# Banded attention and two gated layers on one core: units 8 to 15 of the attention planned 3.5 positions apart instead of 4

## The chip, the cores and the metric

The kernel runs on one core of one Trainium2 chip, in one launch. The metric is device time in microseconds (us): the median of several runs of the whole kernel. One further execution was taken by the hardware profiler, and all rows below come from that one. PE is the matrix engine, PEld its weight loads, DVE the vector engine, ACT the scalar engine, POOL the engine for general work, SP the engine that issues the DMAs.

## The reference

```
k_sum = k.reshape(B, H, nb, 32, D).max(axis=3)
v_sum = v.reshape(B, H, nb, 32, D).mean(axis=3)
scores = concat(where(|i - j| < 16, scale * q @ k.T, -1e9), scale * q @ k_sum.T + log(32))
x = softmax(scores) @ concat(v, v_sum)
x = x.transpose(0, 2, 1, 3).reshape(1536, 512)
x = ((x @ w_a) * (x @ w_b)) @ w_out
h = x @ w_in
out = (h - tanh(h)) @ w_out2
```

B is 2, H 8, S 768 and D 64; the first layer has 1536 inner columns, the second 2048. All is float32.

## The kernel before

**Attention.** The 1536 rows are cut into 24 units of 64 queries, 12 for each batch, all heads at once. A unit goes through T1 (the queries are transposed on PE, line 269, and copied to `qbd` by ACT, line 273), W (its keys are copied, line 280), T2 (scores on PE, line 288; mask and row minimum on DVE, line 299; exponent on ACT, line 303), T2b (normalisation: lines 314, 315 and 317 on DVE for odd units, line 320 on ACT for even ones), T3 (transpose on PE, line 327, copy by ACT, line 330) and T4 (weighted values on PE, line 340; the result is split in a high and a low part by ACT, line 347, and DVE, line 348). Eight units make one block of 512 rows, which the first layer takes as its input tile `XA` (blocks 0 and 2) or `XB` (block 1). Units 0 to 7 run in a hand-written head, units 8 to 15 during block 0 of the first layer, units 16 to 23 during block 1.

**The first layer.** Its work is a list `pos` of positions, 36 for each block. A position is one weight tile of 128 rows by 512 and twelve matmuls: `pos_a` (tile `pa`, line 370, copied to `ta` by ACT, line 378), `pos_b` (tile `pb`, line 370; product `tg` on DVE, line 386; then `gh` on ACT, line 363, and `gl` on DVE, line 364) and `pos_o` (line 398, into four accumulators `acc`). Their order is a0, b0, a1, b1, o0, a2, b2, o1 and so on, and o10, o11 at a block's end. In block 0 position j is the first to use weight j. Of a position's twelve matmuls, some need only the high part of the weight (written by ACT, line 184), the others also the low part (DVE, line 185).

**Weights.** In block 0 every weight is loaded, decoded and split. `load_next` issues a 512 KB load from SP (lines 141 and 143) into one of five staging buffers; `dec_a` reads it on ACT (lines 154 and 155), POOL clamps (line 179), `dec_b` finishes on DVE (lines 161, 164 and 165), and with that the buffer is free and the load of the weight five further on is issued. `split_w` writes the two parts (lines 184 and 185).

**What sets the order.** `plan(j, fn, ...)` hangs a step on position j, and `run_plan(j)` calls it just ahead of that position. From position 0 on, a scheduler orders PE, DVE, ACT and POOL, and calls with T1, T2, T2b, T3, T4, W and `prep_k` in them get a higher priority; SP alone keeps the order in which the steps are called (`REG`). The values of a unit live in three rotating buffers `vw`: with T4 of unit u the plan also calls `load_v(u + 3)` (line 258), which writes the buffer that T4 of unit u reads, so this load waits for that T4, and whatever SP has behind it waits too. `mean_v` (line 240, copied by ACT, line 245) is planned at position 13, the transposes of the second batch's keys (`prep_k`, line 223) at positions 1 to 11.

Of the kernel before, what the change touches and what calls it, by code (L numbers as in the profile page):

```python
# [39 lines left out]
def band_attention_moe_kernel(ctx: ExitStack, tc: tile.TileContext, q, k, v, w_a, w_b, w_out, w_in, w_out2, out):  # L40
# [168 lines left out]
    def where(u):  # L209
        b, w = divmod(u, S // 64)  # L210
        return b, w, min(max(w * 64 - WIN, 0), S - KW)
# [266 lines left out]
    groups, begin, pos = [], {}, []  # L478
# [41 lines left out]
    def plan(j, fn, *args):  # L520
        at.setdefault(j, []).append((fn, args))
# [27 lines left out]
    plan(VM + NC + 4, mean_v, "pt")  # L549
    OFF = -2  # L550
    for n, u in enumerate(range(8, 24)):
        j = (n - 8) * 4 + begin[1] + OFF if n >= 8 else n * (begin[1] // 8) + OFF
        b, w, _ = where(u)
        if u % 2 == 0:
            m = u // 2
            if m + 2 < 12:
                plan(j, load_q, m + 2)
            plan(j, T1, m, "pt", qbd)
            if u >= 12:
                plan(j, W, u)  # L560
                plan(j, W, u + 1)
        if u % 8 == 0:
            plan(j, new_x, u // 8)
        plan(j + 2, T2, u, "ps")
        plan(j + 3, T2b, u)
        plan(j + 5, T3, u, "pt")
        plan(j + 7, T4, u, "ps")
        if u + 3 < 24:
            plan(j + 7, load_v, u + 3)
            if 12 <= u + 3 < 15:  # L570
                plan(max(j + 7, VM + NC + 5), load_vm, u + 3)
# [263 lines left out]
```

## Time and profile before

| what | value |
|---|---|
| median of 3 runs | 660.51 us (659.32 to 661.34) |
| profiled execution, its own time | 659.97 us |
| span in the profile | 658.2 us |
| PE busy | 637.4 us, 97% of the span |
| DVE, ACT and POOL busy | 501.9, 475.1 and 209.1 us |
| granted PE clock, mean | 0.995 |

The span runs from the first instruction to the last; the profiled execution's time holds 1.8 us more, around the span. Matmuls overlap one another, so a busy share of PE near 100% says that PE had work, not that it ran at its peak. A row of the timeline gives the start, the duration, the engine, the line, and in brackets how long the engine stood idle before it and what ended that.

### The profile page before, as it was taken

The page shows a single profiled execution, that of the slowest core. Times are in us where ns is not written, and L with a number is a line of the kernel's source. Part 1 is how long each engine was busy: PE and PEld are TensorE (multiplying, and loading weights), DVE is VectorE, ACT ScalarE, POOL GpSimd, SP SyncE. Part 2 cuts the span into 40 slices and gives each one's busy share as a digit, 9 for nine tenths or more (in the row PEclk, how much of TensorE's full clock was granted, in tenths as well). Part 3 has the DMA queues.
Part 4 walks back from the last instruction along what each step waited for, and adds up shares of the span by engine and source line. Part 5 has one row for each costly group of instructions (what it writes and reads, how often), then busy time and mean ns, then how long its engine had stood idle before and what let it go on. Part 6 is the DMA issues. An engine that isn't in the chain of part 4 may idle for free.

```text
span 658.2 us, 9626 instructions
## 1 busy us (share of the span) xinstructions
PE 637.4 (97%) x3240; PEld 518.2 (79%) x3240; DVE 501.9 (76%) x999; ACT 475.1 (72%) x1000; POOL 209.1 (32%) x221
## 2 busy tenths in 40 slices
PE   7779999999799999999999999999999999999997
PEld 5567876888588888888888888888888888888885
DVE  5889999898675777747877749777777877777775
ACT  4899886897686787645655548777777777777774
POOL 6752231222000011100111134554444554444441
PEclk9979999999999999999999999999999999999999
DMA  9996984563324554513444200000010000010001
GB/s 203 242 240 185 249 224 127 176 214 116 81 89 124 164 161 141 154 54 113 143 145 145 80 1 0 1 0 1 1 64 1 0 1 0 26 40 1 1 0 64
DMA packets 84781, 62.11 MB, mean 94 GB/s; under 512 B 51892, under 2 KB 75444, under 8 KB 84732
## 3 DMA queue, kind: packets, MB, share of 16 engines
q1 hardware_dynamic: 84732, 61.50, 33.3%
q8 instruction: 25, 0.41, 0.3%
q14 instruction: 24, 0.20, 0.1%
HBM read 54.00 MB, written 7.34 MB: 93 GB/s over the span
## 4 chain that ended last, share of the span: by engine, by line
PE 83%; DVE 8%; ACT 4%; DMA 2%; issue 2%; SPq 1%; POOL 0%; DVEq 0%; ACTq 0%
PE acc L459 20%; PE pb L370 18%; PE pa L370 17%; PE acc L398 12%; PE pt L370 5%; PE ps L370 5%; PE ps L288 1%; DVE w L164 1%; PE ps L340 1%; DVE wsp L185 1%; DMA stage<-in_moe_w_in_dram 1%; DVE w L165 1%; PE pt L240 1%; PE pt L327 1%; SPq L610 1%
## 5 line engine op out<-in xcount | busy, mean ns | idle before, releaser
L185 POOL TENSOR_TENSOR wsp<-w,wsp 128x512 fp32r<-128x512 f32 x97 | 127.4, 1330 | 140.0 <-ACT wsp L184 140.0
L184 ACT ACTIVATE wsp<-w 128x512 fp32r<-128x512 f32 x201 | 121.3, 622 | 17.8 <-PE acc L398 8.0
L185 DVE TENSOR_TENSOR wsp<-w,wsp 128x512 fp32r<-128x512 f32 x104 | 73.9, 712 | 41.0 <-ACT wsp L184 40.8
L179 POOL TENSOR_SCALAR w<-w 128x512 f32<-128x512 f32 x52 | 41.8, 809 | 181.7 <-ACT w L154 168.9
L398 PE MATMUL acc<-gh,wsp 128*128 128x512 f32 x288 | 96.5, 394 | 1.2 <-ACT gh L363 1.2
L370 PE MATMUL pa<-XA,wsp 128*128 128x512 f32 x336 | 85.2, 402 | 2.1 <-ACT XA L720 2.1
L370 PE MATMUL pb<-XA,wsp 128*128 128x512 f32 x336 | 83.9, 393 | 1.4 <-DVE tg L386 1.4
L459 PE MATMUL acc<-wsp,gh 128*128 128x512 f32 x256 | 78.8, 389 | 0.0
L370 PEld LDWEIGHTS pa<-XA,wsp 128*128 128x128 f32 x336 | 64.1, 193 | 16.6 <-ACT XA L720 2.4
L370 PEld LDWEIGHTS pb<-XA,wsp 128*128 128x128 f32 x336 | 62.1, 188 | 14.9 <-ACT x21a L155 1.7
L363 ACT ACTIVATE gh<-tg 128x512 fp32r<-128x512 f32 x68 | 42.4, 624 | 33.9 <-DVE tg L386 33.6
L398 PEld LDWEIGHTS acc<-gh,wsp 128*128 128x128 f32 x288 | 53.7, 188 | 11.9 <-ACT gh L363 1.3
L370 PE MATMUL pb<-XB,wsp 128*128 128x512 f32 x240 | 60.8, 396 | 0.0
L370 PE MATMUL pa<-XB,wsp 128*128 128x512 f32 x240 | 60.0, 394 | 0.0
L398 PE MATMUL acc<-gl,wsp 128*128 128x512 f32 x144 | 56.8, 396 | 1.1 <-DVE gl L364 1.1
L459 PEld LDWEIGHTS acc<-wsp,gh 128*128 128x128 f32 x256 | 48.1, 188 | 9.9
L364 DVE TENSOR_TENSOR gl<-tg,gh 128x512 fp32r<-128x512 f32 x68 | 46.8, 688 | 9.1 <-ACT gh L363 8.9
L370 PEld LDWEIGHTS pa<-XB,wsp 128*128 128x128 f32 x240 | 44.5, 188 | 9.4 <-DVE XB L348 0.2
L370 PEld LDWEIGHTS pb<-XB,wsp 128*128 128x128 f32 x240 | 44.4, 188 | 9.2
L459 PE MATMUL acc<-wsp,gl 128*128 128x512 f32 x128 | 49.8, 389 | 0.0
L459 PE MATMUL acc<-wsp,vw 128*128 128x512 f32 x192 | 46.5, 391 | 0.0
L459 PEld LDWEIGHTS acc<-wsp,vw 128*128 128x128 f32 x192 | 35.9, 188 | 8.2 <-ACT vw L363 0.4
(304 smaller groups left out, 1175.5 us busy)
## 6 DMA issues: line engine op xcount, KB each, us to landing
stage<-in_moe_w_out_dram SPq DMA_DIRECT2D x19, 512.0 KB, 3.5
stage<-in_moe_w_in_dram SPq DMA_DIRECT2D x16, 512.0 KB, 5.6
stage<-in_moe_w_a_dram SPq DMA_DIRECT2D x8, 512.0 KB, 5.0
w<-wsc SPq DMA_DIRECT2D x16, 256.0 KB, 3.4
vw<-in_v_dram SPq DMA_DIRECT2D x19, 192.0 KB, 3.0
stage<-in_moe_w_b_dram SPq DMA_DIRECT2D x7, 512.0 KB, 5.6
wsc<-x21a SPq DMA_DIRECT2D x8, 256.0 KB, 5.1
wsc<-x21b SPq DMA_DIRECT2D x8, 256.0 KB, 4.9
```

The source lines that it names most:

```text
L164: nc.vector.scalar_tensor_tensor(r, t[:, :, 1], -0x40000000, r, op0=ALU.bitwise_and, op1=ALU.bitwise_or)
L165: nc.vector.tensor_tensor(r, r, t[:, :, 0], op=ALU.add)
L179: nc.gpsimd.tensor_scalar(rf, rf, HI_HI, HI_LO, op0=ALU.min, op1=ALU.max)
L184: nc.scalar.activation(s[:, 0, :], r, AF.Copy)
L185: eng.tensor_tensor(s[:, 1, :], r, s[:, 0, :].bitcast(F32), op=ALU.subtract)
L240: mm(pp, mavg[:, NB - 4 - 4 * c : 2 * NB - 4 - 4 * c], vch.pop(c).rearrange("p h d -> p (h d)"), start=(c == 0), stop=(c == NC - 1),)
L288: mm(pp[:, p, 0:NK], qt[:, p, :], kw[:, p, :], start=True, stop=True)
L363: nc.scalar.activation(dst[0], src, AF.Copy)
L364: eng.tensor_tensor(dst[1], src, dst[0].bitcast(F32), op=ALU.subtract)
L370: mm(dst, w, xx, start=(kk == 0 and n == 0), stop=(kk == KC - 1 and n == 2))
L398: mm(acc[blk][d][:, c0:c1], w, t, start=(f == 0 and c0 == 0 and n == 0), stop=(f == F1 - 1 and n == 2))
L459: mm(a[c], g[:, cs], s[:, i, :], start=(f == 0 and n == 0), stop=(f == F2 - 1 and n == 2))
```

## The change

Only the position at which the steps of units 8 to 15 are hung changes. `begin[1]` is 36, so the step between them was 36 // 8, that is 4. It is now 3.5, rounded down.

```diff
     OFF = -2
     for n, u in enumerate(range(8, 24)):
-        j = (n - 8) * 4 + begin[1] + OFF if n >= 8 else n * (begin[1] // 8) + OFF
+        j = (n - 8) * 4 + begin[1] + OFF if n >= 8 else n * 7 // 2 + OFF
         b, w, _ = where(u)
```

The starts of units 8 to 15 were -2, 2, 6, 10, 14, 18, 22 and 26; they are now -2, 1, 5, 8, 12, 15, 19 and 22. T2 stands 2 positions after a unit's start, T2b 3, T3 5, T4 and `load_v(u + 3)` 7; T1, W and `load_q` stand at the start. Units 16 to 23 and all else keep their positions.

**SP, loads from the values of unit 14 on.** Rows with `vw<-in_v_dram` are `load_v`; the rows with `moe_w_a`, `moe_w_b` and `moe_w_out` are weights in the order of positions, Before:

```order
L258 DMA vw<-in_v_dram 96x8x64
L263 DMA vw<-w 24x512
L141 DMA stage<-in_moe_w_b_dram 128x4x256
L143 DMA x21a<-in_moe_w_out_dram 128x1024
L141 DMA x21b<-in_moe_w_a_dram 128x4x256
L141 DMA stage<-in_moe_w_b_dram 128x4x256
L258 DMA vw<-in_v_dram 96x8x64
L143 DMA stage<-in_moe_w_out_dram 128x1024
L252 DMA qn<-in_q_dram 128x8x64
L141 DMA stage<-in_moe_w_a_dram 128x4x256
L141 DMA x21a<-in_moe_w_b_dram 128x4x256
L143 DMA x21b<-in_moe_w_out_dram 128x1024
```

Now, from the values of unit 15 on:

```order
L258 DMA vw<-in_v_dram 96x8x64
L252 DMA qn<-in_q_dram 128x8x64
L141 DMA x21b<-in_moe_w_a_dram 128x4x256
L141 DMA stage<-in_moe_w_b_dram 128x4x256
L143 DMA stage<-in_moe_w_out_dram 128x1024
L258 DMA vw<-in_v_dram 96x8x64
L141 DMA stage<-in_moe_w_a_dram 128x4x256
L141 DMA x21a<-in_moe_w_b_dram 128x4x256
L143 DMA x21b<-in_moe_w_out_dram 128x1024
L143 DMA stage<-in_moe_w_out_dram 128x1024
L258 DMA vw<-in_v_dram 96x8x64
L141 DMA stage<-in_moe_w_in_dram 128x4x256 x2
```

Before, the weights of positions 27 to 30 stood behind the values of unit 14, and those of 31 to 34 behind the values of unit 15. Now 29, 30 and 31 stand behind the values of unit 15, 32 to 35 behind those of unit 16, and only weights of the second layer (`w_in`) behind those of unit 17.

**PE, around T4 of unit 15 and the start of block 1.** `XA` marks a matmul of block 0, `XB` one of block 1; line 340 is T4, here of unit 15, line 269 is T1 of units 16 and 17. Before:

```order
L398 MATMUL acc_887<-gl,wsp 128x512
L398 MATMUL acc_887<-gh,wsp 128x512
L327 MATMUL pt<-ident,e 120x128 x4
L340 MATMUL ps<-at,vw 64x64 x8
L269 MATMUL pt<-ident,qn 128x128 x4
L370 MATMUL pa<-XB,wsp 128x512
L370 MATMUL pb<-XB,wsp 128x512
```

Now:

```order
L398 MATMUL acc_890<-gl,wsp 128x512
L398 MATMUL acc_890<-gh,wsp 128x512
L327 MATMUL pt<-ident,e 120x128 x4
L370 MATMUL pa<-XA,wsp 128x512 x2
L340 MATMUL ps<-at,vw 64x64 x8
L269 MATMUL pt<-ident,qn 128x128 x4
L370 MATMUL pa<-XA,wsp 128x512 x10
L370 MATMUL pb<-XA,wsp 128x512 x12
L398 MATMUL acc_887<-gh,wsp 128x512
```

Before, the two `pos_o` rows are o11's and T4 of unit 15 is the last thing ahead of block 1. Now they are o9's: T4 of unit 15 stands inside a11 (position 32), with b11 and o10 behind it; o11 itself stands behind block 1's first twelve matmuls.

**ACT, ahead of the copy of T3 of unit 15 (line 330, tile `at`).** Lines 154 and 155 decode a weight, line 184 splits one. Before:

```order
L184 ACTIVATE wsp_1973<-w_1923 128x512
L184 ACTIVATE wsp_1991<-w_506 128x512
L303 ACTIVATE e_1853,sm_1855<-e_1853,nm_1854 128x120 x4
L184 ACTIVATE wsp_2025<-w_533 128x512
L363 ACTIVATE gh_2021<-tg_2019 128x512
L184 ACTIVATE wsp_2052<-w_609 128x512
L347 ACTIVATE XB_671<-ps_1886 128x4x64
L410 ACTIVATE x20a_2067<-acc0_884 128x512
L410 ACTIVATE x20b_2068<-acc2_886 128x512
```

Now:

```order
L154 ACTIVATE w_1883<-x21a_1723 128x512
L155 ACTIVATE x21a_1723<-x21a_1723 128x512
L303 ACTIVATE e_1740,sm_1742<-e_1740,nm_1741 128x120 x3
L154 ACTIVATE w_1905<-x21b_1777 128x512
L155 ACTIVATE x21b_1777<-x21b_1777 128x512
L347 ACTIVATE XB_671<-ps_1809 128x4x64
L363 ACTIVATE gh_1960<-tg_1958 128x512
L154 ACTIVATE w_1942<-stage_1804 128x512
L155 ACTIVATE stage_1804<-stage_1804 128x512
L184 ACTIVATE wsp_1898<-w_1845 128x512
L155 ACTIVATE stage_1843<-stage_1843 128x512
L330 ACTIVATE at_1853<-pt_1848 120x512
```

Before, no weight of the first layer was left to decode when unit 15 came to its T3. Now the decodes of weights 33 (`w_1883`), 34 (`w_1905`) and 35 (`w_1942`) and one instruction of the first second-layer weight (`stage_1843`) stand ahead of that copy, and the split of weight 32 (`w_1845`) behind all three decodes. Ahead of the first row shown stand, from the decode of weight 32 on, lines 154 and 155 (weight 32), 184 (weight 31), 280 and one of line 303.

## Rows read from the trace of the kernel before

**Rows 1.** Busy time by stretch: us, then busy by engine, clock, DMA share, GB/s.

```profile
57.37:116.52 59.15, 59.15 (x317) 45.36 (x318) 54.83 (x118) 48.27 (x110) 14.10 (x16) 1.00 0.76 197
116.52:176.11 59.59, 56.15 (x321) 45.20 (x320) 52.73 (x124) 49.84 (x118) 12.86 (x15) 1.00 0.47 146
178.01:291.97 113.96, 113.96 (x655) 93.49 (x655) 75.81 (x192) 79.74 (x196) 10.61 (x15) 1.00 0.45 133
```

**Rows 2.** Timeline of PE, end of block 0, from T4 of unit 14.

```profile
168.03 0.69 PE L340 MATMUL ps<-at,vw 120*64 120x64 f32 x16
169.93 1.21 PE L398 MATMUL acc<-gh,wsp 128*128 128x512 f32 x4 [1.21 <-ACT gh L363]
...
176.11 0.69 PE L340 MATMUL ps<-at,vw 120*64 120x64 f32 x16 [1.02 <-ACT at L330]
```

**Rows 3.** Chain of waits in order of time: start, us, what.

```profile
60.35 0.44 PE pt L327 x4
64.47 0.88 PE ps L288 x8
71.76 0.62 PE ps L340 x16
97.46 5.26 PE pt L240 x12
163.81 0.47 ACT at L330
176.79 0.59 PE pt L269 x4
177.38 0.40 PE pa L370
191.20 2.72 PE pa L370 x12
```

**Rows 4.** Timeline around T4 of unit 13: PE, SP, ACT.

```profile
154.47 0.69 PE L340 MATMUL ps<-at,vw 120*64 120x64 f32 x16
155.19 0.33 SPq L258 DMA_DIRECT2D vw<-in_v_dram  x1
155.63 0.48 SPq L143 DMA_DIRECT2D stage<-in_moe_w_out_dram  x1
159.71 0.67 ACT L154 ACTIVATE w<-stage 128x512 f32<-128x512 f32 x1 [0.80 <-DMA stage<-in_moe_w_out_dram]
```

**Rows 5.** Timeline: T4 of unit 10, and the first weight behind it.

```profile
109.24 0.69 PE L340 MATMUL ps<-at,vw 120*64 120x64 f32 x16
115.88 0.67 ACT L154 ACTIVATE w<-x21a 128x512 f32<-128x512 f32 x1 [1.92 <-DMA x21a<-in_moe_w_a_dram]
```

**Rows 6.** Timeline of ACT, back to back.

```profile
149.70 0.51 ACT L280 ACTIVATE kw<-kt 128x384 f32<-128x384 f32 x1
150.11 0.62 ACT L184 ACTIVATE wsp<-w 128x512 fp32r<-128x512 f32 x1
150.63 0.65 ACT L154 ACTIVATE w<-x21b 128x512 f32<-128x512 f32 x1
151.19 0.66 ACT L155 ACTIVATE x21b<-x21b 128x512 int32<-128x512 uint32 x1
151.75 0.38 ACT L303 ACTIVATE e<-e,nm 128x120 f32<-128x120 f32 x1
...
153.26 0.57 ACT L378 ACTIVATE ta<-pa 128x512 f32<-128x512 f32 x1
```

**Rows 7.** Timeline of DVE: the low part of T4 of unit 10.

```profile
111.99 0.42 DVE L348 TENSOR_TENSOR XB<-ps,XB 128x256 fp32r<-128x256 f32 x1
```

**Rows 8.** Busy time by stretch of 2 us; the third number from the end is the clock.

```profile
44.00:46.00 2.00, 2.00 (x6) 1.52 (x6) 1.83 (x4) 1.96 (x5) 0.64 (x1) 0.50 1.39 212
168.00:170.00 2.00, 0.79 (x18) 0.62 (x17) 2.00 (x5) 2.00 (x8) 0.00 (x0) 1.00 0.06 15
```

**Rows 9.** Timeline of PE: the first twelve matmuls of block 0.

```profile
42.48 5.74 PE L370 MATMUL pa<-XA,wsp 128*128 128x512 f32 x12 [2.11 <-ACT XA L720]
```

## The prediction

> **What bounds the kernel now.** I began with busy time by stretch [rows 1]. From 178 us on PE is never idle: in 113.96 us it is busy 113.96, and the chain of waits from there to the end is a string of twelves of matmuls at 2.72 us, one like the next [rows 3]. A change to block 0 therefore moves the end by what PE gains or loses before 178 us, and by nothing more, as long as it opens no wait behind that. From 57.37 to 116.52 PE has no idle time either, though DVE is busy 54.83 of 59.15 us. From 116.52 to 176.11 PE is busy 56.15 of 59.59 us, so 3.44 us are lost. The timeline of PE then says where: all of it lies behind T4 of unit 14 [rows 2]. `o11` waits for `gh` and `gl`, which are made late, and then T4 of unit 15, the last thing that block 1 needs, waits 1.02 us for the copy of its T3 on ACT.
>
> The second thing to read is what starts a weight load. T4 of unit 13 starts at 154.47; the load of values that waits for it is issued at 155.19, the next weight right behind it at 155.63, and ACT, which stood idle for it, begins to decode at 159.71 [rows 4]. So SP's weights stand behind a load that waits for a T4, and the first of them is ready 5.24 us after that T4 starts. After T4 of unit 10 the same took 6.64 us [rows 5]. In block 0 PE can run no further than these weights allow.
>
> **What the change does, and the sum.** It removes and adds no instruction. It moves the steps of units 9 to 15 ahead by 1 to 4 positions against the weights, and the built order shows what comes of that on PE, ACT and SP.
>
> *The wait that goes.* From the start of T4 of unit 14 (168.03) to the first matmul of block 1 (177.38) PE takes 9.35 us [rows 2, 3]. Its work there is T4 twice (0.62 each), `o11` (2.72), T3 (0.44) and T1 (0.59), 4.99 us [rows 3], so 4.4 us are lost. The busy row says 3.44 [rows 1]. The Trainium skill (Perfetto Trace Analysis, Identifying the Most-Contended Engine) says that matmul busy time is a poor measure, since matmuls are pipelined. By the busy row my sum would come out 1.0 us higher; the 4.4 counts starts alone, so I take 4.4 and keep 3.4 as the other end. In the new order `o11` stands behind the first twelve matmuls of block 1, which gives `gh` and `gl` 2.72 us more, and T4 of unit 15 stands in `a11` with 22 more matmuls and `o10` between it and block 1. Both old waits go: -4.4 us.
>
> *The wait that comes.* Now look from T4 of unit 13 to T4 of unit 15 in the new PE order. PE's work between them is T4 0.62, `a10` 2.72, T3 0.44, `b10` 2.72, T2 0.88, T4 0.62, `o9` 2.72, T3 0.44 and two matmuls of `a11` 0.45 (2.72 for twelve): 11.6 us [rows 3]. Behind T4 of unit 13 SP now issues weights 32 to 35, and ACT has to have decoded all four before it splits weight 32 and copies T3 of unit 15. The first lands after 5.24 us [rows 4]. Then ACT takes, by the distance of one start to the next [rows 6]: four decodes of 0.56 + 0.56 each, 4.48; two splits at 0.52, 1.04; W 0.41; four exponents 1.51; `gh`, taken as a split, 0.52; line 347, taken as W, 0.41; one more line 155, 0.56; and the copy of T3, 0.47 [rows 3]. That is 9.4 us, so T4 of unit 15 can start 14.6 us after T4 of unit 13, where PE is ready after 11.6: +3.0 us. Part of it will show a little earlier, at the two matmuls of `a11`, for want of the split of weight 32, or at T3, for want of the normalised rows. The low end is 2.8: from 154.47 to 168.03 PE took 13.56 us [rows 2, 4] for work that sums to 13.27 (T4, two matmuls of `b10`, `o9`, `a11`, T3, `b11`, T2, `o10`), so small work between matmuls costs some 0.3. The high end is 4.4, with 6.64 us for the first landing [rows 5].
>
> *A second wait, at weight 22.* Behind T4 of unit 10 SP now has the values, the queries and then weights 22 to 24, four and more positions ahead of their use where weight 23 was six ahead. PE's work from that T4 to `o6` is two T4, T3, T2, and 46 matmuls: 1.24 + 0.44 + 0.88 + 10.43 = 13.0 us. ACT needs 5.24 + 0.44 for one more issue ahead [rows 4], then three decodes 3.36, three splits 1.56 and 0.1 to the end of the last, W 0.41, `gh` 0.52, exponents 1.51, line 347 0.41: 13.6 us. +0.6 us; between 0 (a load ahead of time) and 2.0 (first landing after 6.64).
>
> *Costed at nothing.* The same sum for weight 29 behind T4 of unit 12 leaves 0.7 us to spare; with the late landing of rows 5 that would be 0.7 lost. `mean_v` keeps its 5.26 us [rows 3] but now stands behind eight matmuls of `o4`, and DVE has the low part of T4 of unit 10 ahead of the decode of weight 19: DVE runs out of work some 5 us before that T4, where it reached this row at 111.99 without such a gap [rows 7]. What hides it is that weight 19 is first needed 6 us of PE work behind that T4; by my estimate it is split about 1 us ahead. If that cover is gone, `o5` waits what is over. The copies of T1, W and the query loads move with their unit, in ACT and SP time that is counted above. In block 1 DVE and ACT are busy 75.81 and 79.74 of 113.96 us [rows 1], so units 16 to 23, which keep their positions and start a little earlier on PE, hide as before.
>
> The sum: -4.4 + 3.0 + 0.6 = -0.8 us. The profiled execution took 659.97 us, 0.54 under the median of the runs, and would come to 659.2; for the median that is 660.51 - 0.8 = **659.7 us**. A measurement of this kernel can tell about 0.3% from no change, 2.0 us, so this is no change. By the bounds alone it lies between -4.4 + 2.8 + 0 = -1.6 and -3.4 + 4.4 + 2.0 + 0.7 = +3.7 us.
>
> **Rivals.** *Faster: one wait goes and little comes.* If the weights behind T4 of unit 13 are ready for ACT sooner than one burst behind a T4 has been so far, or ACT stands ahead by a microsecond, the wait at T4 of unit 15 halves to 1.5 us and the one at weight 22 closes: -2.9 us, 657.6. For it: the old loss was at one place alone, and T4 of unit 15 now has more than two positions in hand before block 1. Against it: ACT's row of decodes is fixed by the order, and no burst in these rows landed faster than 5.24 us. Chance 0.25.
>
> *Slower: SP's queue sets the pace.* SP issues a T4's load of values now 1 to 3 weights earlier, so the bursts of weights start with 3 to 6 positions in hand where they had 4 to 7. If the first weight of a burst takes 6.64 us as behind unit 10 [rows 5], all three places lose: 4.4, 2.0 and 0.7 us, against 4.4 or 3.4 gained: at the upper end +3.7 us, 664.2. It decides from new waits of 6.4 us in sum on. For it: ACT stood idle for the first weight of a burst in both bursts shown. Against it: the 6.64 us held a small copy of `mean_v` between, which stands elsewhere now. Chance 0.18.
>
> *Slower: the clock falls.* In the 2 us from 168 PE was busy 0.79 us and the granted clock stayed 1.00, the 2.4 GHz level; at 44 to 46, after the idle time ahead of the first layer, it was 0.50, which is 1.2 GHz [rows 8]. Twelve matmuls took 5.74 us there [rows 9], 3.0 more than 2.72. One such fall at the new wait gives +2.2 us, 662.7. The Trainium skill (TensorE: Matmul & The Clock Gate, The HAM clock gate) has idle time as what brings the lower level; by that rule the new wait of 3 us would be at risk, and the trace, with longer losses at 1.00, speaks against it. Chance 0.03.
>
> **How the numbers follow.** The forecast has 0.54, all of it within 0.3% of 660.51 (658.5 to 662.5); the first rival is the chance of faster, 0.25; the other two that of slower, 0.21. The likeliest time is 659.7. The range is 657.0 to 663.2: it takes in the first rival's 657.6 with some 0.6 us below it for a weight-22 wait that closes with nothing in its place, the bounds of the sum up to +2.7 us, and leaves out the upper third of the queue rival and the tail of the faster one, under 2 in 10 together.
>
> **What would show it.** Right: the two waits of `o11` for `gh` and `gl` are gone; PE waits for ACT at T4 of unit 15, or just ahead of it at `a11` or T3, some 3 us in sum, two twelves and more before the first matmul on `XB`; that first matmul starts between 173 and 176 us with `o11` still to come; DVE shows a gap of about 5 us ahead of a row of line 348 near 106 to 111 us; SP's weight loads still follow a load of values by 0.4 us; the clock stays 1.00; from 178 us on PE has no idle time. Wrong: no wait of PE over 1.5 us in 150 to 176 (the faster rival), waits of PE in three or more bursts and over 6 us in sum (the slower one), or any wait in block 1, which I have costed at nothing.

## The result, and the profile after

The change makes the kernel slower: 664.86 us median of 7 runs (662.26 to 666.74) against 660.08 of the kernel before beside it (659.02 to 661.34), a ratio of 1.0059 with an interval of 1.0041 to 1.0076 (the quotient of the two medians alone is 1.0072). A second set of 6 runs gave 663.32 and 1.0047 (1.0032 to 1.0063), against 660.46 for the kernel before in that batch. The forecast was 659.7 with a range up to 663.2. With each run below, the ratio is to the kernel before in the same batch, and its interval follows in brackets. One run of one experiment (after_filler), with 804.13 us at a mean granted clock of 0.75, is left out of its median.

First the stretches that answer to [rows 1], in the first profile of the changed kernel (span 665.0 us):

```profile
57.37:116.52 59.15, 58.28 (x311) 44.40 (x312) 50.13 (x111) 46.86 (x108) 12.20 (x16) 1.00 0.72 179
116.52:180.81 64.29, 60.77 (x344) 47.89 (x343) 56.92 (x137) 51.53 (x121) 11.48 (x16) 0.97 0.57 167
181.40:291.97 110.57, 109.21 (x630) 88.87 (x629) 73.35 (x186) 77.26 (x193) 8.94 (x14) 1.00 0.42 122
```

PE is idle 3.52 us in the second stretch, which ends with the start of block 1, about as before (3.44). But 1.36 us are now lost in block 1, where nothing was lost before, the clock of the second stretch is 0.97, and in the first DVE did 50.13 us of work where it did 54.83.

The timeline of PE in that profile has the waits one by one; the rows of T4 are there to place them:

```profile
121.92 0.69 PE L340 MATMUL ps<-at,vw 120*64 120x64 f32 x16
127.15 0.50 PE L398 MATMUL acc<-gh,wsp 128*128 128x512 f32 x1 [1.17 <-ACT wsp L184]
...
154.10 0.69 PE L340 MATMUL ps<-at,vw 120*64 120x64 f32 x16
155.12 0.73 PE L370 MATMUL pa<-XA,wsp 128*128 128x512 f32 x2 [0.33 <-ACT wsp L184]
162.76 0.69 PE L340 MATMUL ps<-at,vw 120*64 120x64 f32 x16
167.31 0.62 PE L327 MATMUL pt<-ident,e 128*120 128x128 f32 x4 [0.92 <-ACT w L154]
168.42 0.73 PE L370 MATMUL pa<-XA,wsp 128*128 128x512 f32 x2 [0.49 <-ACT wsp L184]
169.47 1.02 PE L340 MATMUL ps<-at,vw 120*64 120x64 f32 x16 [0.32 <-ACT at L330]
170.43 1.12 PE L269 MATMUL pt<-ident,qn 128*128 128x128 f32 x4
180.81 1.52 PE L370 MATMUL pa<-XB,wsp 128*128 128x512 f32 x6
277.79 0.62 PE L327 MATMUL pt<-ident,e 128*120 128x128 f32 x4 [1.36 <-DVE e L317]
```

The waits of o11 for `gh` and `gl` [rows 2] are gone, as forecast, and the new wait at T3, a11 and T4 of unit 15 is there. (The bracket at T3 names ACT, but DVE's line 317, which writes the normalised rows of unit 15, ends at 167.17, just ahead of it.) Block 1 starts at 180.81, o11 still to come, where 173 to 176 was forecast. T4 of unit 12 is a row of another kind:

```profile
139.16 0.34 PE L340 MATMUL ps<-at,vw 120*64 120x64 f32 x4
139.43 0.33 PE L269 MATMUL pt<-ident,w 128*128 128x128 f32 x1
139.69 0.33 PE L340 MATMUL ps<-at,vw 120*64 120x64 f32 x2
139.94 0.33 PE L269 MATMUL pt<-ident,w 128*128 128x128 f32 x1
140.21 0.33 PE L340 MATMUL ps<-at,vw 120*64 120x64 f32 x2
140.46 0.33 PE L269 MATMUL pt<-ident,w 128*128 128x128 f32 x1
140.72 0.33 PE L340 MATMUL ps<-at,vw 120*64 120x64 f32 x2
140.98 0.33 PE L269 MATMUL pt<-ident,w 128*128 128x128 f32 x1
141.24 0.45 PE L340 MATMUL ps<-at,vw 120*64 120x64 f32 x6
```

T4 (unit 12) and T1 (units 14 and 15) take turns, matmul by matmul, for 2.4 us; in a row they take 0.62 + 0.59 [rows 3]. No idle time is shown, so no list of waits finds this. The slices of 2 us behind the wait, with the clock as the third number from the end:

```profile
166.00:168.00 2.00, 1.01 (x6) 0.41 (x4) 2.00 (x4) 2.00 (x5) 0.67 (x2) 1.00 1.00 333
168.00:170.00 2.00, 1.26 (x14) 0.82 (x16) 2.00 (x5) 2.00 (x5) 0.00 (x0) 0.91 0.43 147
170.00:172.00 2.00, 2.00 (x16) 1.78 (x13) 2.00 (x5) 1.78 (x4) 0.84 (x1) 0.50 0.12 28
172.00:174.00 2.00, 2.00 (x8) 1.53 (x8) 2.00 (x4) 1.96 (x4) 0.00 (x0) 0.74 0.35 78
```

The clock fell to 0.50, the 1.2 GHz level, and stayed below 1.00 until 174. And DVE stood before the row that [rows 7] showed without a gap:

```profile
106.39 0.70 DVE L364 TENSOR_TENSOR gl<-tg,gh 128x512 fp32r<-128x512 f32 x1
113.14 0.42 DVE L348 TENSOR_TENSOR XB<-ps,XB 128x256 fp32r<-128x256 f32 x1 [6.05 <-ACT XB L347]
```

**Where the time went.** I take the start of each T4 and subtract PE's work since the T4 before it, counted from PE's order at the durations of [rows 3] (0.227 us for a matmul of 512 columns). What is left is lost, whether a row calls it idle or not. Some 0.1 to 0.3 us per unit are usual. Two profiles of each kernel (the second ones are those of the runs below):

| stretch, from T4 to T4 | before | before_again | changed | after_again |
|---|---|---|---|---|
| unit 8 to 9 | -0.20 | -0.21 | 0.29 | 0.29 |
| 9 to 10 | 0.28 | 0.26 | 0.28 | 0.28 |
| 10 to 12 | 0.45 | 0.45 | 2.43 | 1.69 |
| 12 to 13 | 0.29 | 0.29 | 1.53 | 1.53 |
| 13 to 15 | 4.59 | 3.91 | 3.76 | 4.21 |
| 15 to 16 | 0.30 | 0.31 | 1.71 | 1.44 |
| 16 to 23 (block 1) | 1.57 | 1.57 | 3.17 | 1.64 |
| sum | 7.28 | 6.58 | 13.17 | 11.08 |

In all four the span is the start of T4 of unit 8 plus this sum plus 579.3 us, to 0.1 us, so nothing else differs. (Of the experiments' profiles only after_v19late departs from this, by 0.4, and after_filler_2 by the work that it adds.) What the table leaves out is the head: T4 of unit 8 starts at 72.59 in the first profile of the changed kernel and at 71.50 in the second, and at 71.69 and 71.78 before. PE's order is the same in all four up to 72 us, and most of the 1.1 us are there by 17 us. It is a fall of the clock as well, here in the first profile and in the second:

```profile
14.00:16.00 2.00, 2.00 (x12) 2.00 (x11) 0.99 (x5) 0.60 (x2) 0.33 (x1) 0.50 1.17 281
```

```profile
14.00:16.00 2.00, 1.95 (x18) 1.76 (x17) 1.15 (x10) 1.50 (x6) 0.55 (x2) 1.00 1.17 277
```

Nothing that the change moves has run by then. Of the profiles used here, six of the twelve of the changed kernel and its variants have this late head, and none of the four of the kernel before and its variants; whether the change makes it likelier is not shown.

### The profile page after: what moved, and what is told of

Same layout as the page of the kernel before. It is cut to its first block, busy times and chain, and to the rows that moved or that the text cites. A ratio compares the mean times of both kernels' runs of the same rounds, so it can differ in the third digit from the quotient of the medians.

```text
span 665.0 us, 9614 instructions
## 1 busy us (share of the span) xinstructions
PE 642.3 (97%) x3240; PEld 520.4 (78%) x3240; DVE 501.2 (75%) x999; ACT 474.4 (71%) x1000; POOL 204.2 (31%) x221
## 4 chain that ended last, share of the span: by engine, by line
PE 74%; ACT 9%; DMA 8%; DVE 5%; issue 2%; SPq 1%; POOL 1%; DVEq 0%; ACTq 0%; POOLq 0%
PE acc L459 20%; PE pb L370 15%; PE pa L370 14%; PE acc L398 10%; PE pt L370 5%; PE ps L370 5%; DMA stage<-in_moe_w_in_dram 4%; DMA stage<-in_moe_w_out_dram 2%; ACT e L303 2%; ACT stage L155 1%; ACT wsp L184 1%; DMA stage<-in_moe_w_b_dram 1%; PE ps L340 1%; PE ps L288 1%; PE pt L240 1%
## 5 line engine op out<-in xcount | busy, mean ns | idle before, releaser
L179 POOL TENSOR_SCALAR w<-w 128x512 f32<-128x512 f32 x52 | 37.5, 726 | 199.4 <-ACT w L154 184.6
L370 PEld LDWEIGHTS pb<-XA,wsp 128*128 128x128 f32 x336 | 62.1, 188 | 14.6 <-ACT x21a L155 1.7
L155 ACT ACTIVATE stage<-stage 128x512 int32<-128x512 uint32 x47 | 31.6, 673 | 17.9 <-DMA stage<-in_moe_w_in_dram 14.5
```

Of the source, the lines that this page charges most:

```text
L155: nc.scalar.activation(t[:, :, 0], t[:, :, 0].bitcast(U32), AF.Copy, scale=2.0 ** -29)
L179: nc.gpsimd.tensor_scalar(rf, rf, HI_HI, HI_LO, op0=ALU.min, op1=ALU.max)
L370: mm(dst, w, xx, start=(kk == 0 and n == 0), stop=(kk == KC - 1 and n == 2))
```

## The experiments

The theory after the first profile: the loss comes from weights that stand on SP behind a load of values that waits for a T4, and from a clock that falls behind the wait. Its rivals: ACT's own pace, DVE's gap at line 348 of unit 10, and a dense order as such. Where five losses are given below, the stretches are 10 to 12, 12 to 13, 13 to 15, 15 to 16 and 16 to 23. A burst is the weights that stand on SP right behind one load of values.

**The same two kernels again.** No edit.

> The changed kernel once more, to see what of its first profile is there again. In that profile the granted clock fell to 0.50 at 170 to 172 us, behind the small waits ahead of T4 of unit 15, and PE waited 1.36 us in block 1. Theory 'the clock is part of the change': the granted clock falls below 0.8 in some 2 us of 166 to 176 again, and the time is 664 to 667 us. Theory 'queue alone': the waits at weight 22 (1.2 us) and ahead of T4 of unit 15 (1.7 us in sum) are there again, the clock is 1.00 there, and the time of such a run is some 1.7 us lower, 662 to 663.5. Theory 'accident of the head': the first layer's start alone is late in the slow runs, and block 0 and block 1 take what they took before.

> The kernel before once more, beside it on the same chip, for the mean granted clock of each run of both kernels. If the clock is what differs, runs of this kernel show a mean clock higher than those of the changed one by 0.002 to 0.005 (1.3 to 3.3 us of 660) and 659 to 661 us. If the queue alone, the mean clocks of both are alike within 0.001, and the times differ by 3 to 4 us all the same.

663.32 us (1.0047, 1.0032 to 1.0063) and 659.97 us (0.9999, 0.9988 to 1.0011). The mean clock tells nothing: 0.992 to 0.997 over the runs of the one and 0.991 to 0.997 over those of the other, since the head has falls of its own. The profile of after_again shows the same waits (0.88 us at weight 22; 1.70, 0.46 and 0.27 at unit 15), again the clock at 0.50 behind them (168 to 170), and no wait in block 1. So the block 1 wait and the late head of the first profile are not in every run; the rest is in both profiles.

**All loads of values later.**

```diff
-            plan(j + 7, load_v, u + 3)
+            plan(j + 11, load_v, u + 3)
             if 12 <= u + 3 < 15:
-                plan(max(j + 7, VM + NC + 5), load_vm, u + 3)
+                plan(max(j + 11, VM + NC + 5), load_vm, u + 3)
```

> The changed kernel with every load of values planned four positions behind its T4 and no longer beside it. Nothing else moves. Queue theory (weights stand behind a load that waits for a T4): the waits at weights 22, 29 and 32 and at T3 and T4 of unit 15 fall from 3.4 us in sum to under 1 us, the 1.36 us in block 1 go, the clock has nothing to fall behind, and the time is 659 to 661.5. Rival (ACT's own row of decodes, splits and exponents sets the pace of the second half of block 0, whenever the loads come): the wait ahead of T4 of unit 15 stays over 1.2 us, and the time is 663 or more.

> The kernel before with the same edit: every load of values four positions behind its T4. Queue theory: the 4.4 us that PE lost ahead of block 1, where o11 waited for gh and gl, came from the weights behind T4 of unit 13 as well; 2 to 3 us of them go, and the time is 657 to 658.5. Rival: they came from the T3 and T4 of unit 15 standing last, with ACT's copies one behind the other; the time stays within 1 us of 660.

after_vlate took 660.71 us (1.0004, 0.9991 to 1.0016), 2.6 less than the changed kernel. Losses 2.50, 1.52, 0.53, 0.94, 1.33: the end of block 0 is cured (0.53 for 4.21) and the clock does not fall, but the early part is as bad as it was. before_vlate took 656.61 us (0.9949, 0.9932 to 0.9966) and beats both kernels; losses 0.57, 0.05, 1.39, 0.24, 1.41. So most of the old 4.4 us ahead of block 1 came from loads behind a T4 as well; the edit moves all of them at once, so behind which T4 is not shown (behind that of unit 13 stood weight 35 and two of the second layer). The queue theory holds, for the end of block 0. For weight 22 it does not: there waits for DVE remain. And with the queue out of the way in both kernels the change still costs 4.1 us, 660.71 against 656.61: most of it lies from 10 to 12 (2.50 for 0.57) and from 12 to 13 (1.52 for 0.05).

**`mean_v` later.**

```diff
-    plan(VM + NC + 4, mean_v, "pt")
+    plan(VM + NC + 7, mean_v, "pt")
...
-                plan(max(j + 7, VM + NC + 5), load_vm, u + 3)
+                plan(max(j + 7, VM + NC + 8), load_vm, u + 3)
```

> The changed kernel with mean_v planned at position 16 instead of 13 (and load_vm of units 12 to 14 not before 17), so that T4 of unit 10 stands ahead of mean_v on PE again. The weights behind each load of values on SP stay as they are. In the two profiles of the changed kernel DVE stands 6.05 us at line 348 of unit 10, and from T4 of unit 11 to T4 of unit 12 PE loses 1.43 and 2.15 us, where 0.28 is usual. Theory 'DVE gap': that gap is gone, the wait at weight 22 is gone with it (1.15 to 1.9 us), and as the new order also keeps T4 of unit 12 and T1 of units 14 and 15 apart, another 1.1 us go: 660.3 to 661.1. Rival 'queue' (weight 22 is late because it stands behind the values that wait for T4 of unit 10): the gap goes, the wait stays near 1 us, and the time is 662 to 662.5.

661.28 us (1.0011, 0.9998 to 1.0023), 2.0 less than the changed kernel. The weights behind each load of values are the same as in the changed kernel, and the wait at weight 22 is gone: from 10 to 12 it loses 0.73 for 1.69 to 2.43. By itself this does not part the gap from the queue, for with T4 of unit 10 ahead of `mean_v` weight 22 is also issued 19.6 us before o6 starts (108.58 to 128.20), where after_again has 12.7. after_vlate parts them: there it is issued 29.6 us before o6 (99.78 to 129.40), DVE still stands 5.3 us in three waits up to its row of line 348, and 2.50 us are lost. In after_mean16 DVE reaches line 348 of unit 10 without a wait:

```profile
110.04 0.41 DVE L161 TENSOR_SCALAR w<-w 128x512 int32<-128x512 int32 x1
110.38 0.41 DVE L348 TENSOR_TENSOR XB<-ps,XB 128x256 fp32r<-128x256 f32 x1
```

In the changed kernel ACT stands still too. Its copy of `mean_v` (line 245) waits for PE, and the decodes of weights 19 to 21 stand behind it, here in after_again:

```profile
108.94 0.59 ACT L245 ACTIVATE w<-pt 24x512 f32<-24x512 f32 x1 [3.72 <-PE pt L240]
109.43 0.65 ACT L154 ACTIVATE w<-x21b 128x512 f32<-128x512 f32 x1
```

What the gap does to DVE's work is best seen over 20 us, in after_again, before_again and after_vlate in turn:

```profile
100.00:120.00 20.00, 20.00 (x95) 12.99 (x95) 13.45 (x32) 12.04 (x24) 2.56 (x4) 1.00 0.44 123
```

```profile
100.00:120.00 20.00, 20.00 (x107) 14.92 (x106) 18.16 (x44) 13.61 (x30) 3.58 (x5) 1.00 0.57 168
```

```profile
100.00:120.00 20.00, 20.00 (x98) 12.79 (x97) 13.40 (x38) 13.97 (x32) 3.54 (x5) 1.00 0.46 121
```

DVE does 4.7 us less in that window in after_again than in before_again. It had 4.3 us to spare in the 59 us up to 116.52 [rows 1], so what it did not do there comes late, at a weight some 15 us further on. In after_mean16 it does 15.86 us. From 12 to 13 after_mean16 loses 1.19 still, now with a wait of 0.41 at T3, though T4 and T1 stand apart; that part of the expectation failed.

**T1 one position earlier, for units 14 and 15.**

```diff
-            plan(j, T1, m, "pt", qbd)
+            plan(j - (1 if u == 14 else 0), T1, m, "pt", qbd)
```

> The changed kernel with T1 of units 14 and 15 planned one position earlier, which changes one thing: on PE the four transposes of T1 stand ahead of T4 of unit 12 and no longer between its matmuls, one by one. Theory: small matmuls of two kinds in turn cost PE about double; T4 and T1 take 1.2 us and no longer 2.4, and the time falls by 1.1 us against the changed kernel, to 662.2. Rival: PE had that time to lose, since weights and ACT set the pace behind it; then the waits at T3 of unit 15 grow by the same amount, and the time stays at 663.3.

663.21 us (1.0053, 1.0036 to 1.0069). In the profile T1 and T4 of unit 12 stand one behind the other, and 12 to 13 loses 0.28 for 1.53:

```profile
137.13 0.60 PE L269 MATMUL pt<-ident,w 128*128 128x128 f32 x4
137.66 0.69 PE L340 MATMUL ps<-at,vw 120*64 120x64 f32 x16
```

The loss from 13 to 15, 4.07, is that of the changed kernel, so the rival's way of giving it back is not seen. The profiled run took 661.83 us, with a wait of 1.01 in block 1 and no fall of the clock. But the median is that of the changed kernel: with runs from 661.8 to 665.3 the 1.2 us can't be told in the time. Shown in the trace, not in the time.

**Both: `mean_v` at 16 and the loads later.** The two edits together.

> Both edits on the changed kernel: mean_v at 16, and every load of values four positions behind its T4. If the DVE gap and the queue are two causes, the terms add: 663.3 less 2.2 to 3 for the first, less some 2.4 for the waits around T4 of unit 15 and 1.2 for the clock that falls behind them, 656.5 to 658. If they are one cause seen twice, the time is that of the better one alone, 660 to 661.

662.64 us (1.0035, 1.0023 to 1.0047): worse than either alone, which no theory expected. The losses are 3.39, 1.73, 0.53, 1.37, 1.42. With the loads out of the way the scheduler put T3 of unit 12, T2 of unit 13 and T4 of unit 12 nearly one behind the other (128.09 to 132.98), and that T4 waits for a row of line 299:

```profile
132.98 0.69 PE L340 MATMUL ps<-at,vw 120*64 120x64 f32 x16 [1.79 <-DVE nm L299]
```

So this run tells nothing on whether the terms add.

**Work for PE where it waits.** In `pos_o`, behind the twelve matmuls of o9; the profile below is that of after_filler_2, the same kernel.

```diff
+        if (blk, f) == (0, 9):
+            with tc.high_priority(offset=400):
+                for _ in range(5):
+                    mm(acc[blk][3][:, c0:c1], wl, gh, start=False, stop=False)
```

> The changed kernel with five more matmuls of 512 columns right ahead of T3 of unit 15: the last one of o9 once more into the same accumulator (so the sum holds it six times). They are 1.13 us of work in a place where PE waited 0.92 and 1.70 us in the two profiles. Theory 'clock': with PE at work there the granted clock stays 1.00 from 168 to 176, T4 of unit 15 takes 0.7 and not 1.0 to 1.1, and the work costs nothing or gives back up to 1.2 us: 662 to 663.3. Rival 'the clock falls for another reason': it falls all the same, and the time is 663.3 or, where the wait was shorter than the work, up to 664.

> The same edit as in after_filler (five more matmuls of 512 columns ahead of T3 of unit 15, so the accumulator holds one product six times), for its profile alone. Theory 'clock': the granted clock is 1.00 in each 2 us of 164 to 176 and T4 of unit 15 takes 0.7 us. Rival: the clock falls to 0.5 somewhere in 166 to 174 all the same.

663.66 us (1.0054, 1.004 to 1.0068) and 663.94 for the profiled one. The clock holds:

```profile
166.00:168.00 2.00, 1.55 (x10) 1.03 (x8) 2.00 (x4) 2.00 (x4) 0.62 (x1) 1.00 1.02 343
168.00:170.00 2.00, 1.69 (x23) 1.23 (x22) 2.00 (x5) 2.00 (x5) 0.17 (x1) 1.00 0.01 4
170.00:172.00 2.00, 2.00 (x10) 1.63 (x10) 2.00 (x4) 1.77 (x5) 0.71 (x1) 1.00 0.46 103
```

T4 of unit 15 takes 0.69 and not 1.02, and 15 to 16 loses 0.11 for 1.44 to 1.71. That is the price of one fall, 1.3 to 1.6 us, a little more than the 1.13 us that were added. In the time it does not show, and other profiles in which PE lost as much there kept 1.00 (after_t1early, after_v19late). So the clock is a part of the loss in some runs; that it makes the median is not shown.

**One load of values later.**

```diff
-            plan(j + 7, load_v, u + 3)
+            plan(j + (11 if u == 13 else 7), load_v, u + 3)
```

> The changed kernel with one load of values moved: that of unit 16, from beside T4 of unit 13 to four positions behind it. Weights 32 to 35 then stand behind T4 of unit 12 and no longer behind T4 of unit 13; up to T4 of unit 13 PE's order is the same. Queue theory, for the largest term of the forecast: from T4 of unit 13 to T4 of unit 16 PE loses about 1 us and not the 5.5 to 5.7 of the two profiles of the changed kernel, and the time is 663.3 - 4.5 = 659 to 660. Rival: ACT's decodes, splits and copies are too many for that stretch whenever the weights come; PE loses 3 us or more there, and the time is 661.5 or more.

662.09 us (1.0031, 1.002 to 1.0042), 1.2 less and not the 3.3 to 4.3 that the queue theory gave. The waits at T3 and T4 of unit 15 are gone (14 to 16 loses 0.65), but weight 29 is late, by 1.32 us where it was 0.33, and the clock falls behind that. Seven weights now stand behind T4 of unit 12 and not three. Their loads do not slow one another much: from the issue of weight 29 to its decode 5.29 us pass, and 5.13 in after_again. What is new is ACT's order: it decodes weight 32 (152.21, 1.13 us) ahead of the split of weight 29 (154.10).

```profile
154.76 0.73 PE L370 MATMUL pa<-XA,wsp 128*128 128x512 f32 x2 [1.32 <-ACT wsp L184]
155.65 4.14 PE L370 MATMUL pa<-XA,wsp 128*128 128x512 f32 x10 [0.15 <-DVE wsp L185]
```

```profile
154.00:156.00 2.00, 1.08 (x3) 0.60 (x4) 1.78 (x5) 2.00 (x6) 0.66 (x2) 0.98 0.72 201
156.00:158.00 2.00, 2.00 (x6) 1.59 (x5) 2.00 (x5) 2.00 (x5) 0.79 (x2) 0.50 0.60 166
```

Ten matmuls take 4.14 us where twelve take 2.72. So by its own measure this run went to the rival, ACT: from 13 to 16 PE lost 4.31 us, over 3. The weights behind T4 of unit 13 make the wait at unit 15; moved one burst ahead, they make ACT late there.

**Half of the change each.**

```diff
-        j = (n - 8) * 4 + begin[1] + OFF if n >= 8 else n * 7 // 2 + OFF
+        j = (n - 8) * 4 + begin[1] + OFF if n >= 8 else (n * 7 // 2 if n < 4 else n * 4) + OFF
```

```diff
-        j = (n - 8) * 4 + begin[1] + OFF if n >= 8 else n * 7 // 2 + OFF
+        j = (n - 8) * 4 + begin[1] + OFF if n >= 8 else (n * 4 if n < 4 else n * 7 // 2) + OFF
```

> Half of the change: units 8 to 11 stand 3.5 positions apart, units 12 to 15 where they stood before. In its order mean_v stands further ahead of T4 of unit 10, with DVE's decodes of weights 19 and 20 between. If the loss of the change comes from the DVE gap and from the dense end, both are gone and the old waits at the end of block 0 are there: 659.5 to 661. If 3.5 positions among units 8 to 11 cost by themselves, 662 or more.

> The other half: units 8 to 11 where they stood, units 12 to 15 3.5 positions apart. T4 of unit 12 and T1 of units 14 and 15 stand matmul by matmul in turn again, and weights 32 to 35 stand behind T4 of unit 13 again. If the dense end is what costs, it shows the waits ahead of T3 and T4 of unit 15 (2 to 3 us) and 662 to 664; if the loss came from the early half, 659 or less, since the old waits at the end of block 0 are gone.

after_half1 took 663.62 us (1.0054, 1.0035 to 1.0074): the first half alone costs as much as the whole. It loses 4.12 from 10 to 12, in waits for the low part of weights on DVE, and 5.66 from 13 to 15, where the two waits of o11 are back (1.20 and 1.17) and the clock falls to 0.50 behind them (178 to 180):

```profile
132.25 2.37 PE L370 MATMUL pa<-XA,wsp 128*128 128x512 f32 x9 [0.67 <-DVE wsp L185]
142.14 1.20 PE L398 MATMUL acc<-gh,wsp 128*128 128x512 f32 x4 [0.37 <-DVE wsp L185]
144.09 2.57 PE L370 MATMUL pa<-XA,wsp 128*128 128x512 f32 x10 [0.76 <-DVE wsp L185]
```

There `mean_v` stands well ahead of T4 of unit 10, so my account of the gap is not the only way in which denser units 8 to 11 make DVE late. Here it is the queue: weight 22 stands behind T4 of unit 10 (112.37), ACT waits 3.65 us for it, and DVE, which needs what ACT decodes, waits 2.74:

```profile
120.11 0.66 ACT L154 ACTIVATE w<-stage 128x512 f32<-128x512 f32 x1 [3.65 <-DMA stage<-in_moe_w_out_dram]
```

after_half2 took 661.42 us (1.0023, 1.0011 to 1.0035); losses 1.86, 1.53, 2.12, 0.35, 3.23. The dense end costs less than expected; the turns of T4 and T1 and a wait of 1.41 in block 1 are there. From 10 to 12 it loses 1.86 although units 8 to 11 stand where they stood: the scheduler ran `mean_v` later and around T4 of unit 10 there too (104.02 to 110.01), and DVE does 13.86 us of work from 100 to 120, as little as in the changed kernel.

**The terms, taken apart again.** First `mean_v` at 16 with four loads later, then the changed kernel with the loads of block 1 later, then before_vlate at half the distance.

```diff
-            plan(j + 7, load_v, u + 3)
+            plan(j + (11 if 12 <= u < 16 else 7), load_v, u + 3)
```

```diff
-            plan(j + 7, load_v, u + 3)
+            plan(j + (11 if u >= 16 else 7), load_v, u + 3)
```

```diff
-            plan(j + 7, load_v, u + 3)
+            plan(j + 9, load_v, u + 3)
             if 12 <= u + 3 < 15:
-                plan(max(j + 7, VM + NC + 5), load_vm, u + 3)
+                plan(max(j + 9, VM + NC + 5), load_vm, u + 3)
```

> mean_v at 16 as in after_mean16, and the loads of values of units 15 to 18 alone four positions behind their T4; up to T4 of unit 12 PE's order is that of after_mean16. Weights 29 to 32 then stand behind T4 of unit 11, 33 to 35 behind T4 of unit 12, none behind T4 of unit 13. If the DVE gap and the queue at the end of block 0 are two causes whose terms add, PE loses 0.3 and not 2.6 us from T4 of unit 14 to T4 of unit 15, and the time is 661.3 - 2.3 = 659, with up to 0.9 less if weight 29 was late as well. If the dense end costs whatever stands on SP, the time stays over 660.5.

> The changed kernel with the loads of values of units 19 to 23 alone (those that go with T4 of units 16 to 20, in block 1) four positions behind their T4; block 0 stays in the changed kernel's order. Theory 'queue in block 1': the wait of 1.36 us at T3 of unit 23 in block 1, which two of four profiles of that order show at 1.0 to 1.4 us, is gone, and the runs lie closer together and some 0.7 us lower: 662.6. Rival: the wait comes from ACT and DVE; it is there again, and the time stays 663.3.

> The kernel before with every load of values two positions behind its T4, half of the way of before_vlate. If what counts is that a weight stands behind a T4 that is long done, two positions (5.4 us of PE) are about what the first weight behind a T4 took (5.24 us), and the time lies near that of four positions, 656.5 to 658. If each position counts, it lies half way, 658 to 659.

after_mean16_v15late: 660.19 us (1.0009, 0.9997 to 1.0021), which its interval does not part from after_mean16, and which fits neither the 659 nor the 660.5 and more of the two theories. From 13 to 15 it loses 1.35 for 2.86, but from 15 to 16 2.04 for 0.34: the scheduler puts T4 of unit 15 last ahead of block 1 again, and the first matmul on `XB` waits for the copy of it.

```profile
174.75 0.69 PE L340 MATMUL ps<-at,vw 120*64 120x64 f32 x16
177.12 0.50 PE L370 MATMUL pa<-XB,wsp 128*128 128x512 f32 x1 [1.69 <-ACT XB L347]
```

after_v19late: 663.67 us (1.0059, 1.0044 to 1.0073). No wait in block 1 in its profile (1.62 from 16 to 23), as the theory has it, and no gain in the time, which it did not expect; with a wait that only some runs show, one profile does not settle it. before_vlate2: 656.35 us (0.9944, 0.9931 to 0.9956), the same as four positions. It is the best kernel of the study; losses 0.39, 0.27, 1.44, 0.26, 1.41. What is left at the end of its block 0 is one wait:

```profile
172.37 0.69 PE L340 MATMUL ps<-at,vw 120*64 120x64 f32 x16 [0.83 <-ACT at L330]
```

## Why the prediction was wrong

**The wait that goes: right.** Both waits of o11 are gone. The trace of before lost 4.30 and 3.62 us in the two profiles from T4 of unit 14 to that of unit 15; the 4.4 was a fair reading of the first.

**The wait that comes: right in place and kind, a little small.** From T4 of unit 13 to T4 of unit 15 the forecast had 14.6 us; it took 15.37, 15.82 and 15.25 (after_v19late), within the bounds of 2.8 to 4.4 us over PE's 11.6 (by its own numbers the low end is 2.7). ACT began to decode the first weight behind T4 of unit 13 after 5.88 us (at 159.98, having come to it late) and 6.37 us (having waited for it), nearer to [rows 5] than to the 5.24 that I took. That its cause is the queue is shown by after_vlate, where ACT has the same work and 13 to 15 loses 0.53; after_v16late moves the wait, and does not remove it. The two terms were to give 1.4 us and gave next to nothing: 13 to 15 lost 4.59 and 3.91 before, and 3.76, 4.21 and 3.64 after.

**"`mean_v` keeps its 5.26 us ... costed at nothing": this step failed.** The gap on DVE was forecast at 5 us and came at 6.05. The cover that I named, six microseconds of PE work up to weight 19, held for weight 19: o5 has no wait. But it was the wrong thing to ask for. DVE was busy 93% of that stretch before, with 4.3 us to spare, so a gap of 6.05 is not made up, whichever weight stands first behind it; by these two numbers some 1.75 us come out later, as an estimate. They came out at weight 22, where 1.2 and 2.0 us over the usual loss went. Two runs show it together: in after_vlate the queue is out of the way and the loss stays, in after_mean16 the gap is gone and the loss with it. The 0.6 us that I gave to weight 22 for the queue were the right place, and the queue is a smaller part of it: in after_again ACT waits 1.79 us for that weight (to 117.48), but DVE, with 0.39 us of idle time since the gap, comes to it at 121.08.

**A cost that was not seen at all.** The table of starts in the text on the change has T4 of units 8, 10 and 12 at the same positions as T1 of units 10, 12 and 14, which a step of 4 kept apart. PE's built order shows T4 and T1 in turn; the text on the change quotes that order at another place, and I priced no more than what I quoted. That is 1.24 us at unit 12, 1.53 for 0.29 (after_t1early: 0.28), and by the table some 0.5 between T4 of units 8 and 9, where T1 stands ahead of the last two matmuls of T4.

**Weight 29, "0.7 us to spare": none.** From 13 to 14 the changed order loses 0.98 to 1.28 us for 0.29; in the first profile 0.33 of it is a wait for that weight and the rest lies in pieces too short for a bracket. In after_v16late that wait is 1.32.

**The clock, chance 0.03: too low.** I argued from [rows 8] that a longer loss had kept 1.00. In both of the first two profiles it fell, for 1.1 to 1.4 us over the usual loss from 15 to 16. That loss at 1.00 in one profile excludes a fall in the next was my mistake: o11 waited 1.21 and 1.06 us before at 1.00, and behind 1.20 and 1.17 us in after_half1 the clock fell to 0.50. The Trainium skill (TensorE: Matmul & The Clock Gate, The HAM clock gate) has idle time as what brings the lower level. The falls here, each behind waits of PE, agree with it.

**Block 1, "hide as before": not always.** T3 of unit 23 waited 1.36 us in the first profile and 0.66 to 1.41 in three of the experiments' profiles (after_t1early, after_filler_2, after_half2), in others not at all. The queue behind a T4 is not shown to be the cause: after_v19late has no such wait, but neither has after_again, and in the first profile the late load, for which ACT stood 3.18 us up to 267.11, was issued at 261.35, 13.6 us after the last load of values (247.74). The cause stays open.

For the second pair of profiles the table's differences sum to 0.5 (8 to 9) + 1.2 (weight 22) + 1.2 (turns) + 0.3 (13 to 15) + 1.1 (clock) + 0.1 = 4.4 us; the head came 0.3 earlier, and the spans, 661.8 and 657.6, are 4.2 apart. The forecast had 0.8 on the other side, because it priced the waits behind T4 of units 10, 13 and 14 and took the rest as moved without cost. The rival of SP's queue had a time near the result, 664.2, but not by its mechanism: the queue's waits at the end do no more than replace the old ones.

## What to carry to other kernels

When a step is moved past another on one engine, ask what it does on every engine that works in order behind it. Here DVE, busy 93% of the time, stood 6 us, and PE lost 1.2 to 2.0 us some 15 us later, although the first thing behind the gap was in time. After a change of spacing, look at each pair of steps that now falls on the same position: T4 and T1 in turn took 2.4 us here for 1.2, without a wait to show it. And a load that must wait for a buffer belongs at the place in the queue where that buffer is already free: two positions later in the program gave 3.9 us here, five times what the forecast hoped for from the new spacing.

## What the hardware showed that was not expected

In turn, one transpose of T1 or two matmuls of T4 take 0.26 us each time, start to start; in a row four transposes of T1 take 0.36 to 0.59 (0.36 in after_again at 98.03, 0.53 in after_t1early, 0.59 in [rows 3]) and sixteen matmuls of T4 0.62, that is 0.08 for two. Why is not shown. The clock fell behind waits of 1.5 to 2.4 us in sum in four profiles (the first one, after_again, after_v16late, after_half1) and held behind 1.8 to 2.3 in three others (after_mean16, after_v19late, after_t1early), so one profile at 1.00 does not tell that a wait is safe. And runs of one and the same program differ by up to 4.5 us here, by a fall of the clock in the head (1.1 us), one in block 0 and a wait in block 1; each is there or not in the profiles.
